# Six GpSimd buffer clears moved in between the first loads, and one VectorE copy moved behind a row sum, in an attention and MLP kernel

## The chip, the cores and the metric

The kernel runs on one core of a Trainium2 chip. TensorE (PE in the profile) multiplies matrices, VectorE (DVE), ScalarE (ACT) and GpSimd (POOL) work on rows, and SyncE (SP) only issues transfers. The metric is the device time of one execution in microseconds; lower is better. A time is the median of several runs, and the profile is of one execution.

## The reference

```python
def _attn_ref(q, k, v, g_norm):                      # (8, 8, 576, 64): batch, heads, rows, head size
    kv = np.einsum('bhsd,bhse->bhde', k, v)
    out = np.einsum('bhsd,bhde->bhse', q, kv)
    rms = np.sqrt(np.mean(out * out, axis=-1, keepdims=True) + 1e-06)
    return out / rms * g_norm

def _moe_ref(x, g_ln, w_ch1, w_ch2):                 # x: (8, 576, 512), the heads side by side
    mu = np.mean(x, axis=-1, keepdims=True)
    var = np.mean((x - mu) ** 2, axis=-1, keepdims=True)
    xn = (x - mu) / np.sqrt(var + 1e-06) * g_ln
    return x + np.maximum(xn @ w_ch1, 0.0) @ w_ch2   # 512 -> 2048 -> 512
```

Per batch: k and v give one 64x64 matrix per head, q is multiplied by it, each head's row is normalised, and the 512 columns go through a layer norm and two matrix products with a residual.

## The kernel before, in words

**Tiling.** A batch has 576 rows, which makes four tiles of 128 rows ("block b" holds the four tiles of batch b) and 64 rows over. The 64 left over of all eight batches make a ninth block, "rem". In SBUF a batch of q, k or v lies as 128 partitions x 8 heads x 5 slots (`J = 4`, `JJ = 5`): the lower 64 partitions hold five rows each and the upper 64 hold four, so slot 4 of the upper half is empty and has to be zero. There are two buffers of each (`q_in[0..1]`, `k_in[0..1]`, `v_in[0..1]`; batch b uses number b % 2). Batch 0 lies differently: `k_p` and `v_p` are another view of `k_in[0]` and `v_in[0]`, and the first matmuls (`KvFirst`, L250) read them. `kv_pack[b]` (128x512, bf16) takes the per-head matrices of batch b in block-diagonal form, so all of it has to be zeroed beforehand; numbers 0 to 3 are zeroed by VectorE at the start (L164, L170), numbers 4 to 7 by GpSimd (L879).

**Loads.** All loads of q, k, v and of the two weight matrices are issued by GpSimd (`load`, L97 for the lower and L98 for the upper partitions; `load_w1`, L115; `load_w2`, L119), and the transfer casts float32 to bf16. GpSimd runs its instructions in order. Its transfers carry one of eight completion counters in turn, and an issue waits until the transfer that had the same counter eight transfers earlier has landed. The order at the start is: batch 0, the four quarters of the first weight, two 512 KB pieces of the second weight, q, k, v of batch 1 (six transfers), and the last three pieces of the second weight. Then come the clears in `next_memsets` (L877: `kv_pack[4..7]`, then slot 4 of the upper half of `k_in[0]` and of `v_in[0]`), then the loads of k, v, q of batch 2.

**Order of work.** Instructions go to each engine in the order in which the program emits them. TensorE's order is the backbone: block by block the first product (`mm1`, L686) and the second. `tick()` is called about every 1 to 2 us of TensorE work and emits whatever `at(slot, fn)` has put in the agenda at that point; 32 slots stand for one block, and within blocks that use the seven-product form the second half of the slots is squeezed a little. So the slots decide where the work for the next batch (loads, kv matmuls L271, attention tiles L298, turning) stands between the instructions of the current block.

**The second product in seven parts.** In blocks 2 to 7 and "rem", `mm2_seven` computes the second product with seven half-size products (L519) on sums of quarters. VectorE makes the row sums S1, S2, S4, S3 (`row_sums`, L507 to L510) in three pieces, the last of them near the end of `mm1`. In blocks 3 to 7 the products come in the order p1, p4, p6, p5, p2, p3, p7; p6 needs S2 (L508) and writes `p_y`; `scaled_add` (L558, VectorE) reads `p_y`; p3 adds S3 times another weight onto the same `p_y`. GpSimd adds the residual parts (L574, L584, L585, L601).

**Turning q.** `turn_q_dma(b)` copies q of batch b on VectorE into `q_p` (L222) and lets SyncE issue a transposing transfer to `qt` (L224). The attention tiles read `qt`. For batch 1 the same is done in `q_start` (L897, L899), with two of the five slots turned on TensorE (L187). For b of 5 and more the copy stands at slot `32 * b - 47.2`, which for b = 5 is in the second half of block 3. A turned tile of x goes from `xc` (L422) to `xT_blk` through SyncE as well (L433).

Of the kernel before, what the change touches and what calls it, by code (L numbers as in the profile page):

```python
# [14 lines left out]
def kernel(  # L15
# [11 lines left out]
    nc = tc.nc  # L27
# [11 lines left out]
    nDe = Dh // 128  # L39
# [4 lines left out]
    J, JJ, JP = 4, 5, 9  # L44
# [29 lines left out]
    q_in = [consts.tile([128, H, JJ, D], bf16, name=f"q_in{i}") for i in range(NB)]  # L74
    k_in = [consts.tile([128, H, JJ, D], bf16, name=f"k_in{i}") for i in range(NB)]
    v_in = [consts.tile([128, H, JJ, D], bf16, name=f"v_in{i}") for i in range(NB)]
    kv_g = consts.tile([128, HP, 128], bf16)
    kv_pack = [consts.tile([128, HP, 128], bf16, name=f"kv_pack{i}") for i in range(B)]
# [11 lines left out]
    def lo(t, b, h0=0, h1=H):  # L90
        return t[b, h0:h1, :S_LO, :].rearrange("h (p j) d -> p h j d", j=JJ)

    def up(t, b, h0=0, h1=H):
        return t[b, h0:h1, S_LO:, :].rearrange("h (p j) d -> p h j d", j=J)

    def load(dst, t, b, h0=0, h1=H):
        nc.gpsimd.dma_start(dst[:64, h0:h1], lo(t, b, h0, h1))  # L97
        nc.gpsimd.dma_start(dst[64:, h0:h1, :J], up(t, b, h0, h1))  # L98

    def load_batches(slot, what, after):  # L100

        def start(i, name, b):
            if i == 0:
                for element in after():
                    nc.gpsimd.tensor_copy(gate, element)
            dst, src = {"k": (k_in, k), "v": (v_in, v), "q": (q_in, q)}[name]
            load(dst[b % NB], src, b)

        for i, (name, b) in enumerate(what):
            at(slot[i] if isinstance(slot, tuple) else slot, lambda i=i, name=name, b=b: start(i, name, b))  # L110
# [7 lines left out]
    def load_w2(de0, de1):  # L118
        nc.gpsimd.dma_start(  # L119
            w2_sb[:, de0:de1, :],  # L120
            moe_w_ch2[de0 * 128:de1 * 128, :].rearrange("(ko p) n -> p ko n", p=128))
# [49 lines left out]

    load_w2(0, 4)
    load_w2(4, 8)
    for dst, src in ((q_in, q), (k_in, k), (v_in, v)):
        load(dst[1], src, 1)
    load_w2(8, 10)
    load_w2(10, 12)
    load_w2(12, nDe)


    qts, held, blks, rstds, m1s, q_ps = {}, {}, {}, {}, {}, {}
# [28 lines left out]
    def fill(n, p1=None):  # L210
        if p1 is None:
            p1 = ps2.tile([128, 512], f32, tag="p2", name="p1")
        for _ in range(n):
            nc.tensor.matmul(p1, lhsT=fill_sb[:, :128], rhs=fill_sb, start=True, stop=True)
        return p1

    def turn_q_dma(b, j0=0, j1=JJ):
        if j0 == 0:
            q_ps[b] = kv_in.tile([128, JJ, H, D], bf16, tag="qp", bufs=1, name="q_p")
            qts[b] = qt_pool.tile([128, JJ, HP, 128], bf16, tag="qt", name="qt")  # L220
        js = slice(j0, j1)
        nc.vector.tensor_copy(q_ps[b][:, js].rearrange("p j h d -> p h j d"),  # L222
                              q_in[b % NB][:, :, js])
        nc.sync.dma_start_transpose(  # L224
            qts[b][:, js].rearrange("p j hp t -> p (j hp) t"),
            q_ps[b][:, js].rearrange("p j h d -> p (j h d)"))
        if j1 == JJ:
            del q_ps[b]

    def keep_q(b):  # L230

        nc.gpsimd.tensor_copy(qj[:, b], qts.pop(b)[:, J, :, :64])
# [203 lines left out]
    def main_tile(b, j, pool=None, tag="ops"):  # L436
        q_t, kvp = qts[b], held[b]
        if b not in blks:
            blks[b] = new_block()
        return Tile([(slice(0, 128), lambda hp: q_t[:, j, hp, :], kvp)], blks[b], j, pool, tag)  # L440
# [10 lines left out]
    def plan_tile(s, make, turn_at, on_pe, var_at):  # L451
        box = []

        def first():
            t = make()
            box.append(t)
            if t.mms:
                t.o()
            t.sq()
            t.red()  # L460

        def second():
            t = box[0]
            t.y()
            t.x()
            t.xc_w()

        at(s, first)
        at(s + 2, second)
        at(turn_at, lambda: box[0].turn(on_pe))  # L470
        at(var_at, lambda: box[0].var())
# [226 lines left out]
    def rstd_of(b):  # L698
        rstd = work.tile([128, 4], f32, tag="rstd", bufs=3, name="rstd")
        nc.scalar.activation(rstd, blks[b][1][:, 2, :], func=AF.Sqrt, scale=1.0 / Dm, bias=eps_sb)  # L700
        nc.vector.reciprocal(rstd, rstd)
        rstds[b] = rstd
# [56 lines left out]
    def at(slot, fn):  # L759

        i, r = divmod(slot, 32)
        blocks = [*range(B), "rem"]
        if r > 16 and i < len(blocks) and blocks[int(i)] in SEVEN:
            r = 16 + (r - 16) * 14 / 16
        s = sum(30 if x in SEVEN else 32 for x in blocks[:int(i)]) + r
        agenda.setdefault(int(s + 1e-6), []).append((s, fn))

    def tick():
        for _, fn in sorted(agenda.pop(clock[0], []), key=lambda e: e[0]):
# [17 lines left out]
    t = [main_tile(0, 0)] + [main_tile(0, i, *((ps1, "p1"), (ps_m, "misc"), (ps2, "p2"))[i - 1])  # L787
                             for i in range(1, 4)]
# [6 lines left out]
    def part_o(kv_x):  # L795
        hp0, hp1 = kv_x.hps.start, kv_x.hps.stop
        o_0[hp0] = ps_out.tile([128, 2 * (hp1 - hp0), D], f32, tag="ops", name="o_part")
        flat = o_0[hp0].rearrange("p h e -> p (h e)")
        for hp in range(hp0, hp1):
            nc.tensor.matmul(flat[:, (hp - hp0) * 128:(hp - hp0 + 1) * 128],  # L800
                             lhsT=qts[0][:, 0, hp, :], rhs=kv_pack[0][:, hp, :],
                             start=True, stop=True)
# [12 lines left out]
    kv_a.times_g()  # L815
    fill(1)
    kv_b.mms()
    kv_b.copies()
    part_o(kv_a)
    part_o(kv_b)  # L820
# [53 lines left out]
        t[3].x()  # L874
        t[3].xc()

    def next_memsets():  # L877
        for t in kv_pack[4:]:
            nc.gpsimd.memset(t, 0.0)  # L879
        nc.gpsimd.memset(k_in[0][64:, :, J], 0.0)  # L880
        nc.gpsimd.memset(v_in[0][64:, :, J], 0.0)

    at(1, before_1)
    at(2, before_2)
    at(5, lambda: t[2].turn(True))
    at(5.1, before_5)
    at(9.5, next_memsets)
    load_batches(9.6, (("k", 2), ("v", 2), ("q", 2)), lambda: ())
    at(11, lambda: t[3].turn(True))
    for i in range(4):  # L890
# [61 lines left out]


    for b, at_q, at_o in ((3, 56.2, (66.9, 70.7, 74.5, 78.4)), (4, 81, (96.5, 102.7, 109, 115)),
                          *((b, 32 * b - 47.2, tuple(32 * b - i for i in (34.5, 27.3, 20.1, 12.9)))
                            for b in range(5, B))):
        at(at_q, lambda b=b: turn_q_dma(b))
        for j, o in enumerate(at_o):
            plan_tile(o, lambda b=b, j=j: main_tile(b, j), o + 4.5, False, 32 * b - 13.4 + 3.5 * j)
        at(at_o[-1] + .5, lambda b=b: keep_q(b))  # L960
        at(32 * b + 6, lambda b=b: rstd_of(b))
# [63 lines left out]
```

## Time and profile before

| | |
|---|---|
| median of three runs | 278.98 us (278.97 to 279.15) |
| the profiled execution's own time | 279.08 us |
| its span in the profile | 277.0 us |
| PE busy | 269.3 us, 97% |
| DVE busy | 195.4 us, 71% |
| ACT busy | 179.5 us, 65% |
| POOL busy | 101.0 us, 36% |
| granted TensorE clock | full in all 40 slices |

Shares of the span hide stages: the window from 111.0 to 133.2 us, for instance, has VectorE busy for 20.86 of 22.2 us. Views with start times are read in this document as "start, duration, engine, line, operation, tiles, number of instructions, and in brackets how long the engine sat idle before and what ended that". Consecutive instructions of VectorE overlap by a little, since the next begins while the one before drains.

### The profile page before, as it was taken

What the parts mean: (1) busy time and instruction counts of PE and PEld (TensorE: products, weight loads), DVE (VectorE), ACT (ScalarE), POOL (GpSimd) and SP (SyncE); (2) the same over time, 40 slices, a digit from 0 to 9 for tenths busy, and PEclk for the clock granted to TensorE, in tenths of its full rate; (3) what the DMA queues carried; (4) which work ended last, traced back from release to release, by engine and by line L of the source; (5) the groups of instructions that cost most, each with busy time, mean ns of one, the idle gap of its engine ahead of it and who ended that gap; (6) DMA issues with size and microseconds to landing.
All of it is one profiled execution on the core that took longest, in us unless ns stands there. A gap on an engine that the chain in (4) does not pass through costs nothing.

```text
span 277.0 us, 6629 instructions
## 1 busy us (share of the span) xinstructions
PE 269.3 (97%) x2614; PEld 189.6 (68%) x2614; DVE 195.4 (71%) x446; ACT 179.5 (65%) x398; POOL 101.0 (36%) x127
## 2 busy tenths in 40 slices
PE   8799999999999999999999999999999999999994
PEld 2589854996569887458745884588458745874683
DVE  6676448897966894899679856985797469923564
ACT  3667754796448784767677767776777487846610
POOL 8522670016034207901780186017201800180141
PEclk9999999999999999999999999999999999999999
DMA  7999999959985996995399829981611061105032
GB/s 213 199 207 206 197 199 186 265 109 141 193 176 84 189 138 154 160 218 103 42 169 253 140 25 183 241 136 21 161 28 21 20 164 28 21 20 151 2 76 76
DMA packets 65366, 36.80 MB, mean 133 GB/s; under 512 B 35120, under 2 KB 62004, under 8 KB 65336
## 3 DMA queue, kind: packets, MB, share of 16 engines
q0 software_dynamic: 28736, 18.29, 46.4%
q1 hardware_dynamic: 36008, 17.12, 29.8%
q10 hardware_dynamic: 592, 0.98, 1.0%
q8 instruction: 20, 0.33, 0.5%
q14 instruction: 10, 0.08, 0.1%
HBM read 36.71 MB, written 9.44 MB: 167 GB/s over the span
## 4 chain that ended last, share of the span: by engine, by line
PE 81%; DVE 7%; ACT 3%; DMA 2%; issue 1%; DVEq 0%
PE p L686 39%; PE p_z L519 8%; PE p L708 8%; PE p_y L519 7%; PE p_x L519 7%; PE p_s L519 4%; PE p_q L519 3%; PE o_ps L298 2%; PE kv_ps L271 2%; DMA xT_blk<-xc 2%; DVE ss L375 1%; DVE o_ps L379 1%; DVE xc L422 1%; DVE x_blk L397 1%; ACT m L689 1%; DVE o_sb L717 1%
## 5 line engine op out<-in xcount | busy, mean ns | idle before, releaser
L686 PE MATMUL p<-xT_blk,w_sb 128*128 128x128 bf16 (+2 forms) x1024 | 131.6, 286 | 0.6 <-ACT xT_blk L351 0.3
L689 ACT ACTIVATE m<-p 128x512 bf16<-128x512 f32 x144 | 85.5, 596 | 38.6 <-PE p L686 36.1
L686 PEld LDWEIGHTS <-w_sb 128*128 128x128 bf16 x1024 | 78.7, 98 | 45.1 <-issue 1.3
L519 PEld LDWEIGHTS <-m 128*128 128x128 bf16 x448 | 43.3, 98 | 6.6
L375 DVE TENSOR_REDUCE ss<-sq 128x8 f32<-128x512 f32 x35 | 23.8, 680 | 26.1 <-ACT sq L304 26.0
L519 PEld LDWEIGHTS <-S 128*128 128x128 bf16 x344 | 32.9, 98 | 4.2 <-DVE S L508 0.5
L574 POOL TENSOR_TENSOR q<-q,x_blk 128x512 f32<-128x512 f32 x5 | 6.5, 1292 | 70.8 <-ACT q L553 70.8
L708 PE MATMUL p<-w_sb,m 128*128 128x512 bf16 x128 | 29.6, 379 | 0.0
L415 ACT ACTIVATE dev<-x_blk,st_blk 128x512 f32<-128x512 f32 x36 | 25.8, 718 | 1.4 <-DVE st_blk L401 1.4
L379 DVE TENSOR_TENSOR o_ps<-o_ps,inv 128x512 f32<-128x512 f32 x33 | 23.1, 700 | 3.1
L304 ACT ACTIVATE sq<-o_ps 128x512 f32<-128x512 f32 x35 | 20.8, 595 | 5.0 <-PE o_ps L298 5.0
L397 DVE SCALAR_TENSOR_TENSOR x_blk<-o_ps,g_norm_sb 128x512 f32<-128x512 f32 x33 | 22.8, 691 | 1.1
L519 PE MATMUL p_x<-w_sb,m 128*128 128x256 bf16 x192 | 23.4, 273 | 0.0
L708 PEld LDWEIGHTS <-m 128*128 128x128 bf16 x128 | 11.9, 98 | 12.4
L507 DVE TENSOR_TENSOR S<-m 128x768 bf16<-128x768 bf16 (+2 forms) x20 | 11.9, 595 | 11.4 <-ACT m L689 11.4
L383 ACT ACTIVATE rms<-ss,eps_sb 128x8 f32<-128x8 f32 x36 | 10.7, 297 | 13.4 <-DVE ss L375 12.9
L422 DVE TENSOR_SCALAR xc<-x_blk,st_blk 128x512 bf16<-128x512 f32 x32 | 18.0, 563 | 1.1
L601 POOL TENSOR_TENSOR u<-u,x_blk 128x512 f32<-128x512 f32 x6 | 7.6, 1267 | 24.8 <-DVE u L558 24.8
L558 DVE SCALAR_TENSOR_TENSOR u<-p_y,rstd,v 128x256 f32<-128x256 f32 x24 | 10.5, 477 | 6.7 <-PE p_y L519 6.7
L553 ACT ACTIVATE v<-p_x,rstd 128x256 f32<-128x256 f32 x24 | 9.4, 475 | 5.0 <-PE p_x L519 5.0
L390 DVE RECIPROCAL inv<-rms 128x8 f32<-128x8 f32 x36 | 7.1, 196 | 7.8 <-ACT rms L383 7.5
L298 PEld LDWEIGHTS <-qt 128*128 128x128 bf16 x124 | 9.2, 98 | 4.1 <-DMA qt<-q_p 0.5
(146 smaller groups left out, 354.2 us busy)
## 6 DMA issues: line engine op xcount, KB each, us to landing
out_dram<-o_sb SPq DMA_DIRECT2D x24, 256.0 KB, 6.3
w_sb<-in_moe_w_ch_dram POOLq DMA_DIRECT2D x7, 512.0 KB, 13.6
q_in<-in_q_dram POOLq DMA_DIRECT2D x7, 320.0 KB, 5.1
k_in<-in_k_dram POOLq DMA_DIRECT2D x7, 320.0 KB, 7.3
v_in<-in_v_dram POOLq DMA_DIRECT2D x7, 320.0 KB, 10.3
q_in<-in_q_dram POOLq DMA_DIRECT2D x8, 256.0 KB, 8.1
out_dram<-o_sb SPq DMA_DIRECT2D x16, 128.0 KB, 4.5
k_in<-in_k_dram POOLq DMA_DIRECT2D x7, 256.0 KB, 8.0
```

What stands on the lines that cost most here:

```text
L298: nc.tensor.matmul(flat[rows, hp * 128:(hp + 1) * 128], lhsT=lhsT_of(hp), rhs=kvp[:, hp, :], start=True, stop=True)
L304: nc.scalar.activation(self.sq_t, self.o_ps, func=AF.Square)
L375: nc.vector.tensor_reduce(self.ss, self.sq_t, axis=AX.X, op=ALU.add)
L379: nc.vector.tensor_mul(self.o_ps, self.o_ps, self.inv().to_broadcast([128, H, D]))
L397: nc.vector.scalar_tensor_tensor(x_blk[:, ts].rearrange("p (h d) -> p h d", h=H), in0=self.o_ps, scalar=1.0, in1=g_norm_sb.to_broadcast([1 ...
L415: nc.scalar.activation(dev, x_blk[:, ts], func=AF.Square, bias=st[:, 1, ts:ts + 1], accum_out=st[:, 2, ts:ts + 1])
L422: nc.vector.tensor_scalar_add(self.xc_t, x_blk[:, self.ts], st[:, 1, self.ts:self.ts + 1])
L507: for i, fn in enumerate((lambda: nc.vector.tensor_add(S1, a21, a22), lambda: nc.vector.tensor_sub(S2, S1, a11), lambda: nc.vector.tensor_ ...
L519: nc.tensor.matmul(dst[:, t - ts[0], :c1 - c0], lhsT=a[:, i, t * 128:(t + 1) * 128], rhs=w[:, i, c0:c1], start=start and t == ts[0] and i ...
L686: nc.tensor.matmul(p1[:, i, :], lhsT=w1_sb[:, kk, de * 128:(de + 1) * 128], rhs=blk[2][:, kk, sl], start=(kk == 0), stop=(kk == nK - 1))
L689: nc.scalar.activation(m1[:, de0:de0 + per, sl], p1, func=AF.Relu)
L708: nc.tensor.matmul(p2[:, c0:c1], lhsT=m1s[b][:, de, ts * 128:(ts + 1) * 128], rhs=w2_sb[:, de, c0:c1], start=(de == 0), stop=(de == nDe - 1))
```

## The change

Two parts. First, the clears: `next_memsets` goes. GpSimd clears `kv_pack[4..7]` right behind the two 512 KB pieces of the second weight and ahead of batch 1's q; behind that q come the clears in `k_in[0]` and `v_in[0]`, and then k and v of batch 1 and the rest of the second weight. In the program these now stand after batch 0's last kv matmuls, because those read the two buffers. The order of GpSimd's transfers among themselves stays as it was.

Second, the copy of q for batch 5 is put at slot 113.6 in place of 112.8. On VectorE it changes places with one instruction: the S2 sum of the last piece of block 3 (L508) now goes ahead of the copy (L222). On SyncE, the transposing transfer of batch 5's q changes places with one of the `xT_blk` transfers (L433), which now goes first. TensorE and ScalarE have the same instructions in the same order.

```diff
@@ -171,11 +171,9 @@
     load_w2(0, 4)
     load_w2(4, 8)
-    for dst, src in ((q_in, q), (k_in, k), (v_in, v)):
-        load(dst[1], src, 1)
-    load_w2(8, 10)
-    load_w2(10, 12)
-    load_w2(12, nDe)
+    for t in kv_pack[4:]:
+        nc.gpsimd.memset(t, 0.0)
+    load(q_in[1], q, 1)
@@ -815,6 +813,13 @@
     kv_b.mms()
+    nc.gpsimd.memset(k_in[0][64:, :, J], 0.0)
+    nc.gpsimd.memset(v_in[0][64:, :, J], 0.0)
+    load(k_in[1], k, 1)
+    load(v_in[1], v, 1)
+    load_w2(8, 10)
+    load_w2(10, 12)
+    load_w2(12, nDe)
     kv_b.copies()
@@ -874,17 +879,10 @@
-    def next_memsets():
-        for t in kv_pack[4:]:
-            nc.gpsimd.memset(t, 0.0)
-        nc.gpsimd.memset(k_in[0][64:, :, J], 0.0)
-        nc.gpsimd.memset(v_in[0][64:, :, J], 0.0)
-
     at(1, before_1)
     at(2, before_2)
     at(5, lambda: t[2].turn(True))
     at(5.1, before_5)
-    at(9.5, next_memsets)
     load_batches(9.6, (("k", 2), ("v", 2), ("q", 2)), lambda: ())
@@ -952,7 +950,7 @@
-                          *((b, 32 * b - 47.2, tuple(32 * b - i for i in (34.5, 27.3, 20.1, 12.9)))
+                          *((b, 32 * b - (46.4 if b == 5 else 47.2), tuple(32 * b - i for i in (34.5, 27.3, 20.1, 12.9)))
                             for b in range(5, B))):
         at(at_q, lambda b=b: turn_q_dma(b))
```

## The prediction

> **What bounds the kernel now.** I read the page first, then TensorE's instructions in order of time, then the other engines at the two places that the change touches.
>
> ```profile
> PE 269.3 (97%) x2614; PEld 189.6 (68%) x2614; DVE 195.4 (71%) x446; ACT 179.5 (65%) x398; POOL 101.0 (36%) x127
> PE 81%; DVE 7%; ACT 3%; DMA 2%; issue 1%; DVEq 0%
> ```
>
> The first line is busy time, the second the chain of waits that ended last: TensorE is the bound nearly everywhere. So a change pays only where TensorE waits. To find those places I took the start-to-start spacing of its groups against the spacing where nothing holds them (0.109 us for a matmul of 256 columns, from 16 in 1.75 us; 0.216 us for one of 512). From 14.3 us to the end the excess adds up to about 3 us. Most of it lies before 28 us, behind the start's chain through VectorE and ScalarE; 0.24 us lies at 52.8 us, ahead of a kv product; and these two lie in block 3:
>
> ```profile
> 126.63 0.82 PE L519 MATMUL p_y<-T,S 128*128 128x256 bf16 x6
> 127.67 1.27 PE L519 MATMUL p_y<-T,S 128*128 128x256 bf16 x10 [0.23 <-DVE S L508]
> ...
> 132.24 1.05 PE L519 MATMUL p_x<-w_sb,m 128*128 128x256 bf16 x8
> 133.25 1.03 PE L519 MATMUL p_y<-T,m 128*128 128x256 bf16 x8
> ```
>
> Six matmuls from 126.63 should end at 126.63 + 0.66 = 127.29; the seventh starts at 127.67, so p6 waits 0.38 us for S2. Eight from 132.24 should end at 133.11; p3 starts at 133.25, 0.14 us late. VectorE in the same stretch:
>
> ```profile
> 126.13 0.42 DVE L507 TENSOR_TENSOR S<-m 128x512 bf16<-128x512 bf16 x1
> 126.46 0.82 DVE L222 COPY q_p<-q_in 128x2560 bf16<-128x2560 bf16 x1
> 127.20 0.42 DVE L508 TENSOR_TENSOR S<-S,m 128x512 bf16<-128x512 bf16 x1
> 127.65 0.42 DVE L509 TENSOR_TENSOR S<-m,S 128x512 bf16<-128x512 bf16 x1
> 127.99 0.68 DVE L375 TENSOR_REDUCE ss<-sq 128x8 f32<-128x512 f32 x1
> 128.59 1.46 DVE L510 TENSOR_TENSOR m<-m 128x512 bf16<-128x512 bf16 x1
> ...
> 132.32 0.87 DVE L558 SCALAR_TENSOR_TENSOR u<-p_y,rstd,v 128x256 f32<-128x256 f32 x2
> ```
>
> The reader is to see two things. The copy of q stands ahead of S2. And there is no idle time: no bracket on any line from 111.4 us to the L558 at 132.32, which ends at 133.19, 0.06 us before p3 begins. L558 reads the `p_y` onto which p3 adds, so p3 has to wait for it. In this stretch VectorE, not TensorE, is the bound.
>
> At the start, GpSimd and the one VectorE instruction that meets its clears:
>
> ```profile
> 11.14 0.69 POOL L97 DMA_DIRECT2D q_in<-in_q_dram  x1 [0.29 <-DMA q_in<-in_q_dram]
> 13.76 0.68 POOL L98 DMA_DIRECT2D q_in<-in_q_dram  x1 [1.92 <-DMA w_sb<-in_moe_w_ch_dram]
> 16.03 0.68 POOL L97 DMA_DIRECT2D k_in<-in_k_dram  x1 [1.59 <-DMA q_in<-in_q_dram]
> ...
> 31.36 1.94 POOL L879 MEMSET kv_pack<- 128x512 bf16 x4
> 33.35 1.09 POOL L880 MEMSET k_in<- 64x512 bf16 x1
> 34.39 1.06 POOL L881 MEMSET v_in<- 64x512 bf16 x1
> 35.41 0.87 POOL L97 DMA_DIRECT2D k_in<-in_k_dram  x1
> ```
> ```profile
> 31.72 2.26 DVE L897 COPY q_p<-q_in 128x2560 bf16<-128x2560 bf16 x1 [4.54 <-DMA q_in<-in_q_dram]
> ```
>
> GpSimd waits between its first loads for counters to come free, and the clears run behind them, 4.05 us long, ahead of batch 2's loads.
>
> **Part 2, the copy behind S2.** Nothing is added; two neighbours change places on VectorE and two on SyncE. L508 has to wait for L507's result, 0.46 us start to start (as 127.20 to 127.65), so it runs from 126.59 to 127.01, before TensorE's need at 127.29: minus 0.38 us at p6. The copy follows at 126.59 + 0.33 = 126.92, and L509 at 126.92 + 0.74 = 127.66, against 127.65 before. From there VectorE's queue is what it was: L510 at 128.60, L558 until 133.20. TensorE now reaches p3 at 133.11 - 0.38 = 132.73 and stands there until 133.26. The 0.38 us that p6 gives, p3 takes: what is late next is L558, and the sum of part 2 is +0.01 us. L510's length enters this: it is 1.46 us where the same sum takes 0.41 us in later blocks, because GpSimd's L574 began at 128.49, 0.10 us before it. L574 hangs on ScalarE's work on p4, which is over before p6, so it stays at 128.49 and L510 stays behind it.
>
> On SyncE the `xT_blk` transfer goes ahead of batch 5's q. Its `xc` is there at 126.2, so it issues until about 127.6 (1.27 us), and the q transfer follows at 127.8 in place of 127.31. Turning takes 4.9 us to landing, so it lands at 132.7. The tile that reads it starts at 134.12: covered by 1.4 us. The next `xT_blk` transfer (132.43, landing 2.4 us later) waits for its `xc` anyway and is needed at 136.96.
>
> **Part 1, the clears.** Taken away behind the loads: 4.05 us of GpSimd. Added ahead of q: four clears, 1.94 us, from 10.86 to 12.80; q's lower half is issued at 12.80 in place of 11.14, its upper half at 13.76 as before (it waits for a counter). Then two clears: the rows say 1.09 and 1.06 us, but these lay beside VectorE's copy and scaling; by the kv_pack rows of 0.49 us each for as many elements per partition, 14.44 to 15.42. Upper bound 16.55. k's lower half comes at 16.03 to 16.6, and all later issues wait for their counters as before. Their wait for batch 0's kv matmuls (last start 10.17) is over by then.
>
> Does the later issue of q's lower half cost? It landed 19.2 us after its issue, at 30.3, the one before it at about 29. Transfers land in order and the traffic is level at about 200 GB/s from 8 to 50 us: 12.80 is still 16 us ahead of its turn. Nothing.
>
> Do the earlier loads of batch 2 gain? They now wait for counters: issues at about 31.7, 33.1, 34.4, 36.0, 37.5, 38.5 in place of 35.41 to 39.16. But they landed 10.9 to 16.1 us after issue, behind others in the same stream, the last at 55.3. Kv of batch 2 at 52.83 had its v at 50.7. Bounds: nothing, and at best the 0.24 us at 52.8, which the chain puts down to ScalarE's L431 behind VectorE's continuous work since 41.8 us. I take nothing.
>
> The copy L897 of batch 1's q: 0.82 us without the clears (six rows of L222), so it ends up to 1.44 us earlier, and so does the transposing transfer, which lands at 46.0 in place of 47.4. Its reader's weight load waited 0.29 us at 47.45, but TensorE's matmul there begins at 47.49, on its natural spacing. Nothing, or up to 0.06 us.
>
> What the clears meet in their new place: VectorE's chain of the first tiles, on which TensorE waits. Lower bound nothing: products and reductions with a float32 or PSUM operand kept their length beside GpSimd's work (L375 0.69 us at 109.54, L558 0.88 us for two at 108.70, as elsewhere). Upper bound: the bf16 `diag` (L328, at 15.85) or the copy at 16.48 is held. I take nothing, since the clears are over at 15.42.
>
> The row for such a hold is L897: 2.26 us, of which 33.98 - 0.82 = 33.16 is the start if it ran undivided, just when the four clears end. The Trainium skill, "SBUF — State Buffer", section "Who interferes with whom", speaks against putting clears here: VectorE's fast copies and scalings between bf16 buffers and GpSimd's instructions take one shared port pair as an exclusive lock, and whichever starts second is blocked until the first ends. By that rule L897 would have ended at 31.36 + 1.94 + 0.82 = 34.12; the trace has 33.98 and agrees. By the same rule `diag` is open to a hold by one clear and the work on PSUM around it is not: the sum would be 0 with clears of 0.49 us, and C below with clears of 1.09.
>
> **Sum.** The profiled execution's 279.08 us (2.08 around its span) + 0.01 + 0 = 279.09; that execution lies 0.10 above the median, so the median to expect is 279.0 us.
>
> **Rivals.** A, the gain stays: L558 is not what p3 waits for. The 0.06 us between them speaks against it. 278.98 - 0.38 = 278.60.
>
> B, L510 slips ahead of L574. Then VectorE is 1.05 us earlier, L558 is done by 132.2, and both waits go: 0.38 + 0.14 = 0.52, 278.46. It takes 0.10 us less on VectorE or more on ScalarE; in blocks 4 and 5 L510 did come first.
>
> C, slower: `diag` is held at the start. It decides if the two clears take over 0.7 us each, so that they still run at 15.85. With 1.09 and 1.06 they end at 16.55; if the load's issue behind them holds VectorE too (the `xc` at 113.36 took 1.33 us in place of 0.49 beside load issues, while scaling at 37.43 kept its 0.81), `diag` ends at 17.23 + 0.25 = 17.48. TensorE needs it at 16.74: 0.1 to 0.74 us, up to 279.72.
>
> D, slower: batch 1's turning, 1.44 us earlier, slows the stream ahead of the last piece of the second weight, which landed at 44.2 and is first read at 43.81 + 4 x 0.216 = 44.67. Slack 0.47; the delay at most 1.44, the remaining slowdown in the stream about 0.5. Cost 0.03 to 0.97, 279.0 to 279.95.
>
> E, faster: A or B, and the 0.24 us at 52.8 as well: 278.2 to 278.4.
>
> **How the numbers follow.** A measurement of this kernel can tell about 0.2%, 0.56 us: 278.42 to 279.54. Forecast 0.46; A 0.13 (0.02 beyond); B 0.14 (0.08 beyond, it lies at the edge); E 0.06, all beyond; C 0.13 (0.10 beyond); D 0.08 (0.05 beyond). Faster 0.16, slower 0.15, same 0.69. The range from 278.3 to 279.6 leaves out half of E, half of C and a little of D; the forecast's own is 278.8 to 279.2.
>
> **What would show it.** Right: the bracket at p6 is gone, p3 starts about 0.5 us after its turn and 0.06 us behind L558; L897 near 0.82 us; clears at 10.9 and 14.4; load landings up to 55.3 unchanged. Wrong: L510 at 0.42 us (B), p3 on its spacing (A), the first `mm1` or the turning at 16.6 late (C), a gap at 44.67 (D).

## The result and the profile after

| | before | after |
|---|---|---|
| median | 279.02 us (278.84 to 279.76, 22 runs) | 279.43 us (279.06 to 280.06, 22 runs) |
| ratio after / before | | 1.0015 (95% interval 1.0009 to 1.0021) |
| the profiled execution, its span | 279.08, 277.0 us | 279.31, 277.3 us |

The changed kernel is 0.4 us slower. That is below the 0.2% that the prediction called the least a measurement can tell, though with this many runs the interval leaves 1 out. The forecast was 279.0 us, in the range 278.3 to 279.6. The rise is small but real, so the question is where 0.4 us came from when the sum said 0.01.

In the changed kernel most line numbers are two lower (before's L519 is L517, L558 is L556, L508 is L506, L510 is L508, L222 is L220, L897 is L895). TensorE after, in order of time:

```profile
126.55 1.91 PE L517 MATMUL p_y<-T,S 128*128 128x256 bf16 x16
...
131.77 1.05 PE L517 MATMUL p_x<-w_sb,m 128*128 128x256 bf16 x8
133.16 1.03 PE L517 MATMUL p_y<-T,m 128*128 128x256 bf16 x8 [0.35 <-DVE u L556]
134.39 0.40 PE L296 MATMUL o_ps<-kv_pack,qt 128*128 128x128 bf16 x4 [0.20 <-ACT dev L413]
```

p6 runs its sixteen matmuls in one group: its wait is gone. The eight matmuls from 131.77 are over at 131.77 + 0.87 = 132.64, and p3 starts at 133.16, so p3 waits 0.52 us. Then comes what the prediction did not have: eight matmuls of p3 from 133.16 are over at 134.03, and the next instruction, the first attention tile of batch 5, starts at 134.39, 0.36 us late. The bracket names ScalarE, the last event before it; the weight load that has to come first names the wait that counts:

```profile
134.39 0.23 PEld L296 LDWEIGHTS <-qt 128*128 128x128 bf16 x4 [0.47 <-DMA qt<-q_p]
```

The tile waits for the turned q of batch 5. In the trace's completion events that transfer is issued at 127.70 and its last part lands at 134.34, 6.64 us later. Before, it was issued at 127.31 and landed at 134.01, and the tile's weight load started at 134.05: no bracket, but also no slack.

```profile
134.05 0.27 PEld L298 LDWEIGHTS <-qt 128*128 128x128 bf16 x4
```

VectorE after:

```profile
126.51 0.42 DVE L506 TENSOR_TENSOR S<-S,m 128x512 bf16<-128x512 bf16 x1
126.85 0.82 DVE L220 COPY q_p<-q_in 128x2560 bf16<-128x2560 bf16 x1
127.59 0.42 DVE L507 TENSOR_TENSOR S<-m,S 128x512 bf16<-128x512 bf16 x1
...
128.52 1.44 DVE L508 TENSOR_TENSOR m<-m 128x512 bf16<-128x512 bf16 x1
...
132.24 0.87 DVE L556 SCALAR_TENSOR_TENSOR u<-p_y,rstd,v 128x256 f32<-128x256 f32 x2
```

S2 and the copy have changed places with the predicted spacing (0.34 and 0.74 us), and from L507 on the queue is that of before to within 0.1 us, the long L508 (before's L510) included.

The clears after, on GpSimd, and the two VectorE instructions that they could meet:

```profile
10.70 1.96 POOL L175 MEMSET kv_pack<- 128x512 bf16 x4
...
14.18 0.52 POOL L816 MEMSET k_in<- 64x512 bf16 x1
14.64 0.52 POOL L817 MEMSET v_in<- 64x512 bf16 x1
```
```profile
15.74 0.25 DVE L326 TENSOR_SCALAR diag<-identity,st_blk 128x128 bf16<-128x128 bf16 x1
...
31.23 0.83 DVE L895 COPY q_p<-q_in 128x2560 bf16<-128x2560 bf16 x1 [4.17 <-DMA q_in<-in_q_dram]
```

The two later clears take 0.52 us each, not the 1.09 and 1.06 of before, and are over at 15.16, ahead of `diag`, which keeps its 0.25 us (before, it ran at 15.85). The copy of batch 1's q, freed of the clears, takes 0.83 us in place of 2.26.

### The profile page after: what moved, and what is told of

Its sections match the earlier page's. It is cut to its first block, busy times and chain, and to the rows that moved or that the text cites. A ratio compares the mean times of both kernels' runs of the same rounds, so it can differ in the third digit from the quotient of the medians.

```text
span 277.3 us, 6630 instructions
## 1 busy us (share of the span) xinstructions
PE 269.4 (97%) x2614; PEld 189.6 (68%) x2614; DVE 193.2 (70%) x446; ACT 179.4 (65%) x398; POOL 99.9 (36%) x127
## 4 chain that ended last, share of the span: by engine, by line
PE 93%; DMA 3%; ACT 2%; DVE 1%; issue 1%; POOLq 0%
PE p L684 44%; PE p L706 10%; PE p_x L517 8%; PE p_z L517 8%; PE p_y L517 7%; PE p_s L517 4%; PE p_q L517 4%; PE o_ps L296 3%; DMA v_in<-in_v_dram 3%; PE kv_ps L269 2%; ACT m L687 1%; PE tp L198 0%; PE p L212 0%; ACT xT_blk L429 0%; PE tp L427 0%
## 5 line engine op out<-in xcount | busy, mean ns | idle before, releaser
L517 PEld LDWEIGHTS <-m 128*128 128x128 bf16 x448 | 43.3, 98 | 7.0 <-issue 0.5
L517 PEld LDWEIGHTS <-S 128*128 128x128 bf16 x344 | 33.0, 98 | 3.7
L517 PE MATMUL p_x<-w_sb,m 128*128 128x256 bf16 x192 | 23.4, 273 | 0.0
L556 DVE SCALAR_TENSOR_TENSOR u<-p_y,rstd,v 128x256 f32<-128x256 f32 x24 | 10.4, 477 | 6.7 <-PE p_y L517 6.7
L517 PE MATMUL p_y<-T,m 128*128 128x256 bf16 x96 | 11.9, 272 | 0.3 <-DVE u L556 0.3
```

Of the source, the lines that this page charges most:

```text
L517: nc.tensor.matmul(dst[:, t - ts[0], :c1 - c0], lhsT=a[:, i, t * 128:(t + 1) * 128], rhs=w[:, i, c0:c1], start=start and t == ts[0] and i ...
```

## The experiments

The theory after the result: the rise is the wait of batch 5's first tile for its q, which lands late because the copy, and so the issue, comes 0.4 us later. Rivals: the clears cost something that the other parts of the profile hide; SyncE's new order, not the copy, delays the transfer; or p3's wait alone is the loss.

All runs are judged by one more view besides their time. Without any wait, the stretch from p6's first matmul to the first matmul of the `p_z` group that follows the tile takes 8.07 us (the last kernel below). What it takes beyond that is TensorE's loss around the change. It is the sum of three waits, each a start less the natural end of the group before (0.109 us per matmul of 256 columns, 0.755 us for the kv group of 40). Around the stretch little differs: in the eight profiles of the table, what lies before it takes 126.47 to 126.74 us and what lies behind it 141.80 to 141.87, so the other parts of the profile hide no loss or gain larger than these ranges.

| kernel | stretch, us | beyond 8.07 | p6 | p3 | tile | q issued, landed |
|---|---|---|---|---|---|---|
| before | 8.58 | 0.51 | 0.38 | 0.14 | 0 | 127.31, 134.01 |
| after | 8.95 | 0.88 | 0 | 0.52 | 0.36 | 127.70, 134.34 |
| clears alone | 8.58 | 0.51 | 0.42 | 0.09 | 0 | 127.35, 133.96 |
| copy alone | 8.98 | 0.91 | 0 | 0.52 | 0.40 | 127.74, 134.40 |
| copy, SyncE's order of before | 8.84 | 0.77 | 0 | 0.52 | 0.26 | 127.91, 134.43 |
| after, tile later | 8.57 | 0.50 | 0 | 0.53 | 0 | 127.83, 134.44 |
| after, addition later | 8.91 | 0.84 | 0 | 0.02 | 0.84 | 127.63, 134.23 |
| after, both later | 8.07 | 0 | 0 | 0 | 0 | 127.83, 134.37 |

### The clears alone

The changed kernel with the copy of q back in its old slot:

```diff
-  *((b, 32 * b - (46.4 if b == 5 else 47.2), tuple(...))
+  *((b, 32 * b - 47.2, tuple(...))
```

> The clears alone (the copy of batch 5's q stays at slot 112.8). Theory Q (the changed kernel is slower because batch 5's first tile waits for its turned q, which part 2 makes late): level with the kernel before, ratio 0.9995 to 1.0005, TensorE 0.38 us late at p6 and 0.14 at p3 as before. Theory C (the clears, or the earlier turning of batch 1, cost the time): about 0.4 us slower, ratio 1.0015.

Measured: 279.03 us beside 279.09 for the kernel before, ratio 0.9998 (0.999 to 1.0007).

```profile
127.71 1.26 PE L517 MATMUL p_y<-T,S 128*128 128x256 bf16 x10 [0.26 <-DVE S L506]
```

p6 is cut in two by its wait for S2 again, and the tile follows p3 without a wait. The clears cost and give nothing that can be measured.

### The copy alone

The kernel before with the copy of batch 5's q one slot later:

```diff
-  *((b, 32 * b - 47.2, tuple(...))
+  *((b, 32 * b - (46.4 if b == 5 else 47.2), tuple(...))
```

> The moved copy alone (the clears stay behind the loads). Theory Q: the whole of the rise, ratio 1.0010 to 1.0020, no wait at p6, about 0.5 us at p3, and some tenths more at the first tile of batch 5, ended by the landing of the turned q. Theory C: level with the kernel before, since p6's gain and p3's wait cancel.

Measured: 279.40 us, ratio 1.0015 (1.0007 to 1.0024).

```profile
134.44 0.23 PEld L298 LDWEIGHTS <-qt 128*128 128x128 bf16 x4 [0.51 <-DMA qt<-q_p]
```

The whole rise is there without the clears, with the same wait.

### The copy behind S2, SyncE in its old order

At slot 113.45 the copy still follows S2 on VectorE, but the q transfer goes out ahead of the `xT_blk` transfer, as before:

```diff
-  *((b, 32 * b - 47.2, tuple(...))
+  *((b, 32 * b - (46.55 if b == 5 else 47.2), tuple(...))
```

> The moved copy alone, at slot 113.45 in place of 113.6: VectorE's order as in the changed kernel, SyncE's order as before (the turning of batch 5's q ahead of the xT_blk transfer). If the place on SyncE is what makes q late: the tile waits less, 0 to 0.2 us in place of 0.36, ratio about 1.0005. If the copy's own 0.4 us is what makes it late, or the transfer lands after the one behind it as it did in the kernel before (134.01): the tile waits as long or longer, ratio 1.0010 to 1.0020. Theory C: level with the kernel before.

Measured: 279.43 us, ratio 1.0016 (1.0007 to 1.0024). The tile still waits, 0.26 us, which lies between the two outcomes that were expected. Here, as before and after the change, q is issued 0.03 us after its copy ends, whichever transfer goes first: the copy ends at 127.88 and q is issued at 127.91 here, 127.28 and 127.31 before, 127.67 and 127.70 after. So the order on SyncE doesn't delay the issue; the place of the copy on VectorE is enough. The stretch is 0.11 us shorter than after the change, but it begins 0.19 us later in this profile (126.74 against 126.55), and the time shows no gain.

### The tile half a slot later

If the tile's wait is the rise, a tile that comes behind all sixteen matmuls of p3 should take it away, and leave p3's wait:

```diff
-  tuple(32 * b - i for i in (34.5, 27.3, 20.1, 12.9))
+  tuple(32 * b - i for i in (34 if b == 5 else 34.5, 27.3, 20.1, 12.9))
```

> The changed kernel with batch 5's first tile half a slot later, behind p3's last matmuls (0.87 us more for its q to land). Theory Q: the wait at the tile is gone and the scatter with it, level with the kernel before, ratio 0.9995 to 1.0005; p3 still waits 0.5 us. Theory C: as the changed kernel, ratio 1.0015.

Measured: 279.07 us, ratio 0.9999 (0.999 to 1.0008).

```profile
133.28 1.91 PE L517 MATMUL p_y<-T,m 128*128 128x256 bf16 x16 [0.35 <-DVE u L556]
135.02 0.39 PE L296 MATMUL o_ps<-kv_pack,qt 128*128 128x128 bf16 x4
```

p3 waits as in the changed kernel, the tile doesn't wait, and the time is that of before. This is the sum that the prediction made, p6's 0.38 us handed to p3 and nothing else, as a kernel of its own.

### The addition later: rival B on purpose

Rival B said that the time falls if the S3 sum (L508 after) comes before GpSimd's addition to q. Here that addition of block 3 is put behind the addition to `u`, so it can't overlap the sum:

```diff
         scaled(q, p_q, 1)
-        add(q, q, x(1, 0))
+        if b == 3:
+            late.append(lambda: G.tensor_add(q, q, x(1, 0)))
+        else:
+            add(q, q, x(1, 0))
```

> The changed kernel with GpSimd's addition to q in block 3 (L574 of the kernel before) put behind its addition to u, so that it does not hold VectorE's L510. If p3 waits for VectorE's queue, and the tile for q: L510 takes 0.42 us in place of 1.44, p3's wait of 0.52 us is gone, and the tile takes it over, about 0.9 us in place of 0.36, since q lands when it did; the whole as the changed kernel, ratio 1.0010 to 1.0020. If p3 waits for something else: p3's wait stays. If the tile's wait is not set by q's landing: about 0.5 us faster than the changed kernel, ratio 0.9995.

Measured: 279.31 us beside 279.01, ratio 1.0016 (1.0007 to 1.0025). VectorE and TensorE:

```profile
128.44 0.42 DVE L508 TENSOR_TENSOR m<-m 128x512 bf16<-128x512 bf16 x1
...
131.26 0.87 DVE L556 SCALAR_TENSOR_TENSOR u<-p_y,rstd,v 128x256 f32<-128x256 f32 x2
```
```profile
132.57 1.04 PE L517 MATMUL p_y<-T,m 128*128 128x256 bf16 x8
134.28 0.40 PE L296 MATMUL o_ps<-kv_pack,qt 128*128 128x128 bf16 x4 [0.67 <-DMA qt<-q_p]
```

The sum (L508) falls from 1.44 to 0.42 us, L556 comes 0.98 us earlier, and p3 starts on its spacing (131.68 + 0.87 = 132.55). So far this is B. But the tile is now due at 132.57 + 0.87 = 133.44 and q lands at 134.23: it stands for 0.84 us and takes all of p3's gain. By this profile B's price of 278.46 was never to be had while the tile stood in its place.

The fall from 1.44 to 0.42 us also tells what made the sum long. This is GpSimd's addition in the changed kernel:

```profile
128.41 1.27 POOL L572 TENSOR_TENSOR q<-q,x_blk 128x512 f32<-128x512 f32 x1 [10.46 <-ACT q L551]
```

It ran from 128.41 to 129.68, and the sum ended at 128.52 + 1.44 = 129.96. The Trainium skill, "SBUF — State Buffer", section "Who interferes with whom", says that a VectorE instruction with two SBUF inputs contends with a GpSimd instruction that reads SBUF, and that the port pair which they share is an exclusive lock. If the addition holds that lock from start to end, the sum ends at 129.68 + 0.42 = 130.10; the trace agrees to 0.14 us, the same difference as for the copy at 31.72 before.

### Both later: all three waits away

The two edits above together, on the changed kernel.

> The changed kernel with both: batch 5's first tile behind p3, and GpSimd's addition to q behind its addition to u in block 3. Theory Q with the queue on VectorE: both waits are gone, p6's gain of 0.38 us and p3's 0.14 are kept, 0.4 to 0.5 us faster than the kernel before, ratio 0.9981 to 0.9986. If the late addition makes GpSimd late for the loads of batch 6 or for o_sb, some of it comes back there.

Measured: 278.59 us beside 279.01, ratio 0.9987 (0.9978 to 0.9995).

```profile
132.78 1.91 PE L517 MATMUL p_y<-T,m 128*128 128x256 bf16 x16
134.52 0.39 PE L296 MATMUL o_ps<-kv_pack,qt 128*128 128x128 bf16 x4
```

No bracket is left, and the stretch gives 8.58 - 8.07 = 0.51 us against before; the median falls by 0.42 us. This version is faster than both kernels, by 0.13% over the one before. It has no room: the tile's weight load starts at 134.41 and q lands at 134.37.

### Why q's landing takes 6.6 us: TensorE's instruction transfer

Before and after the change, the turnings of batches 2, 3, 6 and 7 take 4.8 to 5.1 us from issue to landing, and batch 4's takes 5.5 and 5.0. Batch 5's takes 6.5 to 6.7 in every kernel of the table. In the changed kernel 15 of its 16 completions come by 132.66, and the last at 134.34; in the kernel before, all 16 come from 133.79 to 134.01. What lies there is a 16 KB transfer of kind "instruction", 0.9 us long, at 131.99 before and 132.20 after. There are 20 of them in the run, about one for each 261 TensorE instructions (2614 matmuls and as many weight loads), and they are taken here to be TensorE's own.

The trace's packet records show where q waits. The turnings of batches 2, 3, 6 and 7, before and after, end with 32 packets of 4 bytes, all of which start 4.1 to 4.5 us after the issue. In batch 5's turning, in all eight kernels of the table, 30 do, and the last two start in the last 0.02 us of the instruction transfer (133.06 and 133.07 after the change, where it ends at 133.08). The instruction transfer itself starts 4.5 to 4.7 us after q's issue in all eight, so a later copy still means a later landing.

To move the instruction transfer, this kernel (with the copy moved, without the clears) has more instructions on TensorE at the start: 72 small matmuls in place of 14 of the 18 warm-up matmuls, whose result is used nowhere.

```diff
-    fill(18)
+    small = fill(4)
+    for _ in range(72):
+        nc.tensor.matmul(small[:, :8], lhsT=fill_sb[:, :128], rhs=fill_sb[:, :8], start=True, stop=True)
+    del small
```

> The moved copy alone, with 14 of TensorE's 18 warm-up matmuls at the start replaced by 72 of 8 columns (58 more matmuls, so TensorE comes to each 16 KB of its instructions earlier; the warm-up's result is used nowhere). This moves the 0.9 us instruction transfer that lay at 132.0 to 132.4 us, on top of batch 5's turning, to about 126. Theory F (that transfer holds one part of the turned q back): q lands 4.8 to 5.2 us after its issue as in the other blocks, not 6.6, the first tile of batch 5 does not wait, and what block 3 loses against the kernel before is 0. Rival (this turning takes 6.6 us for another reason): it lands after 6.6 us and the tile waits 0.4 us as before. The start may be some tenths longer or shorter, so the whole time says less than the trace here.

Measured: 282.4 us, ratio 1.0132 (1.0108 to 1.0155). The time is spoilt by the edit itself: block 3 lies some 3.4 us later. Of that, 1.1 us is the start (the first `mm1` comes at 15.93 us in place of 14.80), 0.8 us a kv product's wait for v at 74.40, and 1.3 us the wait of batch 3's first tile for its q at 85.50. Only the turnings of q and the stretch in block 3 are read from this run. The DMA rows between issue and landing (packets, MB, share of 16 engines), first of the changed kernel (127.7 to 134.4), then of this one (131.0 to 136.1):

```profile
q1 hardware_dynamic: 3407, 0.85, 66.0%
q8 instruction: 1, 0.02, 0.8%
```
```profile
q1 hardware_dynamic: 2997, 0.75, 76.7%
```

The instruction transfer has moved to 128.11 (about 126 was expected), ahead of q's issue at 131.16. All 32 small packets go out by 4.4 us after the issue, and q lands at 136.02, 4.86 us after it. The tile's weight load has no wait, and the stretch takes 8.58 us with p3's 0.53 us as its only wait, as in the kernel with the later tile:

```profile
137.37 0.32 PEld L298 LDWEIGHTS <-qt 128*128 128x128 bf16 x4
```

The same edit brought instruction transfers onto turnings that had landed in time before: at 61.02, 83.60 and 189.89, 4.5 to 4.6 us after the issues of batches 2, 3 and 7. These three now take 6.52, 6.32 and 6.55 us, and the second of them is the 1.3 us wait at 85.50. For batches 2 and 7 the last two small packets again start as the instruction transfer ends. For batch 3 all 32 are out by 4.45 us, just ahead of the instruction transfer at 4.46, and 14 of the 16 completions are late all the same.

Lying there is not enough by itself. In the kernels with the copy alone, with the addition later and with both later, an instruction transfer also starts 4.5 to 4.7 us after batch 2's issue, but all 32 small packets are out by 4.4 us, and q lands after 4.9. So for batch 5 the delay is that the instruction transfer gets ahead of the last two small packets. Why the last completion comes another 1.3 us after these packets (134.34 against 133.07), and what holds batch 3's in this run, is not shown.

## Why the prediction was right, and where it was not

- **p6's gain.** Predicted 0.38 us; the bracket is gone, and the wait was 0.38 to 0.42. Right.
- **p3 takes it.** Predicted: p3 stands 0.53 us, until L558 is done. Measured 0.52 to 0.53 in all kernels with the copy moved, until the addition was put later. Right, and the kernel with the later tile gives this sum alone: 279.07 us.
- **L510 stays behind L574.** 1.44 us. Right; with the addition out of the way it takes 0.42.
- **The clears cost nothing.** Right in time (279.03 alone), and the row that was chosen for their length held: 0.52 us each, nearest to the 0.49 of the `kv_pack` rows, so `diag` at 15.74 is not held. C would have needed over 0.7.
- **The loads and L897.** L897 at 0.83, as predicted. The last issue of batch 2's loads comes at 40.14, where 38.5 was predicted, without effect. D happened in miniature: the last piece of the second weight lands at 44.7 (44.2 before), the twelve matmuls from 43.70 take 2.75 us to the next group in place of 2.59, and 0.10 of that 0.16 us is given back at 52.8, where the wait shrinks from 0.24 to 0.14.
- **The q transfer, the step that failed.** The prediction wrote: "Turning takes 4.9 us to landing, so it lands at 132.7. The tile that reads it starts at 134.12: covered by 1.4 us." Issue was right (127.70 for 127.8). The landing was wrong: 4.9 is the median that the profile's DMA row gives for the turnings, and this one took 6.70 us in the very trace that was being read (127.31 to 134.01). Over all seven turnings the completion events give a median of 5.1; 4.9 comes out only without the two whose landing the profile's row doesn't tell, batch 4's (5.54 us) and this one. With its own figure it lands at 134.4 to 134.5, against a tile due at 134.12, and the sum is +0.3 to +0.4, 279.3 to 279.4. The missing term is the 0.36 us at the tile.
- **The rivals.** A did not occur. B was named as the other way to gain, but its price left out the same landing. None of the rivals had the wait at the tile, though "what is late next" was the question of that part; it was asked of p3 and not of the tile behind it.

The forecast of no change that can be told stands, and so does the range, but for the time as a whole that is in part luck. The missed term, 0.36 us, happened to be smaller than the 0.56 us that the prediction took as the least that can be told; and 279.43 lies above the 278.8 to 279.2 that the prediction gave the forecast itself, in the part of the range that had been left for C and D, which were not the cause.

## What to carry to other kernels

A work item that is moved down a full queue delays every reader of its result: follow its own consumers to the end, not only the ones that wait now. Take a transfer's duration from that very transfer in the trace, not from the median of its kind, and compare its landing with the start of its reader: a reader without a wait may have 0.04 us of slack. Where several waits stand in a row, removing one only shows the next; the gain came when all three were gone (0.51 us in the stretch, 0.42 us in the time), while each edit short of that gave nothing or a loss.

## What the runs showed that was not expected

A transfer of instructions, 16 KB and 0.9 us long, can hold back the end of a transposing transfer: of 32 small packets the last two start only as it ends, and the turning lands 6.5 to 6.7 us after its issue in place of 4.8 to 5.1. That was seen for batch 5 in eight kernels and for batches 2 and 7 in the ninth. Adding 58 matmuls at the start moved the transfer that met batch 5's q from 132.4 to 128.1 us, while block 3 came 3.4 us later, and so put it ahead of q.
